# Scores of two items in every second slot, with 6 and 10 MLP pieces by turns

## The chip, the cores and the metric

The kernel runs on one core of one Trainium2 chip. The time is the device time of one execution in microseconds (us): 1641.6 us before, the median of 3 runs (1641.4 to 1641.78). The core has five engines that run side by side, each through its own list of instructions in order: TensorE (PE, matmuls; PEld are its weight loads), VectorE (DVE), ScalarE (ACT), GpSimd (POOL) and SyncE (SP, DMA issues). They wait for each other by semaphores. Matmul results land in PSUM[...]; ScalarE or VectorE copies them on to SBUF.

## The reference, cut to what matters

Attention that keeps only the 32 largest scores of each row, over 8 batches, 8 heads, 576 positions and a head size of 64, and then an MLP with exact gelu on the 4608 resulting rows. Everything is fp32.

```python
def _attn_ref(q, k, v):                       # (8, 8, 576, 64) each
    scores = scale * np.matmul(q, k.transpose(0, 1, 3, 2))
    kth = np.partition(scores, -32, axis=-1)[..., -32:-31]
    scores = np.where(scores >= kth, scores, -1e9)
    scores = scores - np.max(scores, axis=-1, keepdims=True)
    attn = np.exp(scores)
    attn = attn / (np.sum(attn, axis=-1, keepdims=True) + 1e-09)
    return np.matmul(attn, v)

# x = attention output as (4608, 512)
def _moe_ref(x, w_in, w_out):                 # (512, 2048), (2048, 512)
    h = x @ w_in
    g = 0.5 * h * (1.0 + erf(h / np.sqrt(2.0)))
    return g @ w_out
```

## The kernel before

The attention is cut into 144 items. An item is 128 query rows of two heads; 18 items make a batch, and two of these 18 hold the last 64 rows of the heads. The main loop has one slot for each item (and four more), and the stages of an item lie in successive slots:

- its scores: matmuls into `t_ps` (the last 64 keys of both heads) and `s_ps` (the first 512 keys, two banks), and ScalarE copies both into the item's row tile `s`;
- two slots later the top 32 of each row on VectorE, four rounds of eight;
- in the slot after that the masked softmax on ScalarE (prelu, then exp with its sum), the inverse of the sum on VectorE and the normalising on GpSimd;
- in the slot after that the transposes on TensorE, which ScalarE copies to `pt`; and for every second item one slot later the product with v (`o`), for both items at once.

The MLP is cut into 1152 pieces, each four recorded matmuls into `h_ps` (first layer) or two into `y_ps` (second layer), and these pieces are laid between the attention's work. `block` gives eight pieces of one layer, and blocks of the layers alternate. A gelu of two tiles follows each block of the second layer. The excerpts are in the order of the file; `...` marks cuts.

```python
    def scores(i):
        ...
        S_of[i] = s = work.tile([P, 2 * S], f32, tag="s", bufs=5, name="s")
        s_ps = ps.tile([P, 2, 512], f32, tag="s", bufs=1, name="s_ps")
        t_ps = ps.tile([P, 512], f32, tag="tp", name="t_ps")      # two buffers of tag "tp"
        if t < NM:
            ...
            nc.tensor.matmul(t_ps[:, 0:P], lhsT=lhsT, rhs=qk[:, SM + P : KT], start=True, stop=True)
            for c in range(2):
                for e in range(2):
                    ...                        # 64 rows of the array: one head each
                    nc.tensor.matmul(s_ps[:, e, c * 256 : (c + 1) * 256], ...)
            ...
            nc.scalar.activation(spread(s, S + TL, SM), s_ps, func=AF.Copy, scale=scale)
            nc.scalar.activation(s[:, SM : S + TL], t_ps[:, 0:P], func=AF.Copy, scale=scale)
        ...

    def top_k(i, hooks):
        ...
        for r in range(TOPK // 8):
            for e in range(2):
                nc.vector.max(st["top"][:, e, 8 * r : 8 * r + 8], cur[e])
            if r < TOPK // 8 - 1:
                ...                            # match_replace, both heads
            if r in hooks:
                hooks.pop(r)()
    ...
    def softmax(i, e):
        ...
        nc.scalar.activation(s, s, func=AF.Prelu, bias=st["neg"][:, e, 1:2], scale=1.0, alpha=STEEP)
        nc.scalar.activation(s, s, func=AF.Exp, bias=st["bias"][:, e : e + 1], scale=1.0,
                             accum_out=st["den"][:, e : e + 1])

    def transposes(i):
        ...
        def tails():                           # reads the ends of both heads' rows
            ...
                nc.tensor.transpose(tp[:, 0:P], s[:, SM : S + TL], ident)
                nc.scalar.copy(out=pt_now[0][:, 2 * NM, ...], in_=tp[:, 0:P])
        def main(e):                           # four transposes of one head's row
            ...
            nc.scalar.copy(out=dst, in_=tp.rearrange("p (j n) -> p j n", j=NM))

        return [tails] + [lambda e=e: main(e) for e in range(2)]
```

The loop over the slots. `mlp(k)` issues up to k pieces, as long as the slot's allowance `left[0]` lasts. `prep` are transposes that prepare q and k of a later pair of heads; not all slots have them.

```python
    ahead = N + 4                              # N = 144 items
    for n in range(ahead):
        left[0] = 4 if n in (START, START + 1) else 8        # START = 10
        ...
        scores(n + 2)
        product = attend(n - 3)                # o: product with v, for every second item
        late = n > START
        ...
        copy_x()                               # ScalarE copies o
        mlp(1)
        tr = transposes(n - 2)
        if product and n > START and ...:      # the next piece needs the rows of this product
            for piece in tr[:1]:
                piece()
            tr, ready[0] = tr[1:], n_tok[0]
        if n > START:
            softmax(n - 1, 0)
        mlp(1)
        ...
        mlp(1)
        prep = prep_in.pop(n, [])
        if len(prep) > 1 and len(tr) == 3:
            tr, prep = tr[:1] + prep[:1] + tr[1:], prep[1:]
        for piece in tr[:-1]:                  # tails and the first main
            piece()
            ready[0] = n_tok[0]
            mlp(1)
        ...
        if late:
            softmax(n - 1, 1)
        add_small(n - 1)                       # GpSimd: den + 1e-9
        ...
        for piece in tr[-1:] + prep:           # the second main, preparation
            piece()
            mlp(1)
        run_gelus()
        mlp(left[0])                           # what is left of the allowance
        run_gelus()
        if n < N:
            top_k(n, {3: lambda: inverse(n - 1)})     # VectorE: 1/den behind the top-k
        ...
        threshold(n)                           # GpSimd: neg, bias
        ...
        normalise(n - 1, 2 if on_pool(u) else 0)      # GpSimd, both heads; VectorE in a few early slots
```

Of the kernel before, what the change touches and what calls it, by code (L numbers as in the profile page):

```python
# [14 lines left out]
def kernel(  # L15
# [6 lines left out]
    w_out: bass.AP,  # L22
    out: bass.AP,
):

# [7 lines left out]
    nc = tc.nc  # L35
    f32, i32, u32 = mybir.dt.float32, mybir.dt.int32, mybir.dt.uint32
    bf16, i16, u16 = mybir.dt.bfloat16, mybir.dt.int16, mybir.dt.uint16
    AF = mybir.ActivationFunctionType
    ALU = mybir.AluOpType

    B, H, S, D = q.shape
    P = 128
# [3 lines left out]
    NP = H // 2  # L46
    NM = S // P
    SM = NM * P
    TL = S - SM
# [174 lines left out]
    N = len(items)  # L224
# [35 lines left out]
    def spread(t, step, n):  # L260

        return bass.AP(tensor=t.tensor, offset=t.offset, ap=[list(t.ap[0]), [step, 2], [1, n]])

    def half(r, e):


        return slice((r ^ e) * TL, ((r ^ e) + 1) * TL)
# [2 lines left out]

        return spread(t[:, e * TL :], step + (TL if e == 0 else -TL), TL)

    def scores(i):
        if i >= N:
            return
        pair, t = items[i]
        S_of[i] = s = work.tile([P, 2 * S], f32, tag="s", bufs=5, name="s")
        s_ps = ps.tile([P, 2, 512], f32, tag="s", bufs=1, name="s_ps")
        t_ps = ps.tile([P, 512], f32, tag="tp", name="t_ps")
        if t < NM:  # L280
            qk = qk_of[pair]
            lhsT = qk[:, t * P : (t + 1) * P]
            nc.tensor.matmul(t_ps[:, 0:P], lhsT=lhsT, rhs=qk[:, SM + P : KT], start=True, stop=True)  # L283
            for c in range(2):
                for e in range(2):
                    rows = slice(e * D, (e + 1) * D)
                    nc.tensor.matmul(  # L287
                        s_ps[:, e, c * 256 : (c + 1) * 256], lhsT=lhsT[rows, :],
                        rhs=qk[rows, KT + c * 256 : KT + (c + 1) * 256], start=True, stop=True,
                    )  # L290
            if i == 0:

                nc.scalar.activation(s[:, 0:SM], s_ps[:, 0], func=AF.Copy, scale=scale)  # L293
                nc.vector.tensor_scalar(s[:, SM : S + TL], t_ps[:, 0:P], scale, None, op0=ALU.mult)
                nc.scalar.activation(s[:, S + TL :], s_ps[:, 1], func=AF.Copy, scale=scale)  # L295
                return
            nc.scalar.activation(spread(s, S + TL, SM), s_ps, func=AF.Copy, scale=scale)  # L297
            nc.scalar.activation(s[:, SM : S + TL], t_ps[:, 0:P], func=AF.Copy, scale=scale)
        else:
            for r in range(2):  # L300
                qk = qk_of[pair + r]
                for e in range(2):
                    nc.tensor.matmul(
                        t_ps[half(r, e), r * TL : (r + 1) * TL],
                        lhsT=qk[:, SM + e * TL : SM + (e + 1) * TL],
                        rhs=qk[:, SM + P + e * TL : SM + P + (e + 1) * TL],
                        start=True, stop=True,
                    )

            for r in range(2):  # L310
                qk = qk_of[pair + r]
                for e in range(2):
                    rows = slice(e * D, (e + 1) * D)
                    nc.tensor.matmul(  # L314
                        s_ps[half(r, e), r, :], lhsT=qk[rows, SM + e * TL : SM + (e + 1) * TL],
                        rhs=qk[rows, KT:], start=True, stop=True,
                    )
            s2 = s.rearrange("p (r n) -> p r n", r=2)
            nc.scalar.activation(s2[:, :, 0:SM], s_ps, func=AF.Copy, scale=scale)
            nc.scalar.activation(  # L320
                s2[:, :, SM:S], t_ps[:, 0:P].rearrange("p (r n) -> p r n", r=2),
                func=AF.Copy, scale=scale,
            )

    def top_k(i, hooks):

# [47 lines left out]
    def softmax(i, e):  # L374

        if i < 0 or i >= N:
            return
        st, s = stat_of[i], row(i, e)
        nc.scalar.activation(s, s, func=AF.Prelu, bias=st["neg"][:, e, 1:2], scale=1.0, alpha=STEEP)  # L379
        nc.scalar.activation(  # L380
            s, s, func=AF.Exp, bias=st["bias"][:, e : e + 1], scale=1.0,
            accum_out=st["den"][:, e : e + 1],
        )
# [56 lines left out]
    def copy_x():  # L440
        while copies:
            copies.pop()()

    n_tok, read = [0], [0]

    copies = []

    def attend(i):

        if i < 0 or i >= N:  # L450
            return False
        pair, t = items[i]
        b, at = divmod(pair, NP)
        if t < NM and t % 2 == 0:
            return False
        pt = pt_now[0]
        o = ps.tile([P, 512], f32, tag="tp", name="o")
        n, row = (2 * P, (t - 1) * P) if t < NM else (TL, SM)
        tok = place_of(b, row)
        assert read[0] >= tok + n - RING  # L460
        c = slice(tok % RING, tok % RING + n)
        if t < NM:
            vt = raw_of("v", pair)
            for j in range(NJ):
                for e in range(2):
                    nc.tensor.matmul(  # L466
                        o[e * D : (e + 1) * D, 0:n], lhsT=vt[:, j, e, :],
                        rhs=pt[:, e * NM + j if j < NM else 2 * NM, :],
                        start=(j == 0), stop=(j == NJ - 1),
                    )  # L470
            copies.append(lambda: nc.scalar.copy(out=xT[:, at, c], in_=o[:, 0:n]))
        else:
            for r in range(2):
                vt = raw_of("v", pair + r)
                for j in range(NJ):
                    for e in range(2):
                        nc.tensor.matmul(  # L477
                            o[e * D : (e + 1) * D, r * TL : (r + 1) * TL], lhsT=vt[:, j, e, :],
                            rhs=pt[:, r, j, half(r, e)], start=(j == 0), stop=(j == NJ - 1),
                        )  # L480
            copies.append(lambda: nc.scalar.copy(
                out=xT[:, at : at + 2, c],
                in_=o[:, 0 : 2 * TL].rearrange("p (r n) -> p r n", r=2),
            ))

        if t == (NM if b % 2 == 0 else NM - 1):
            for r in range(2 if t == NM else 1):
                load("v", pair + r + NP + 1)
        if at == (NP - 1 if t < NM else NP - 2):
            assert n_tok[0] == tok  # L490
            n_tok[0] = tok + n
        return True

# [135 lines left out]
    for pair in range(2):  # L631
        for piece in transpose_qk(pair, pair == 0):
            piece()
        if pair == 0:
            scores(0)
            scores(1)

# [6 lines left out]
    for pair in range(2, n_pairs):  # L646
        b, p = divmod(pair, NP)
        for at, piece in zip(first.get(pair, slots_of[b % 2][p]), transpose_qk(pair)):
            prep_in.setdefault(starts[b] + at, []).append(piece)
    ahead = N + 4  # L650
    for n in range(ahead):

        left[0] = 4 if n in (START, START + 1) else 8
        eager[0] = n > N
        weights_add(unit_in(n))
        scores(n + 2)
        product = attend(n - 3)
        late = n > START
        if n <= START:

            softmax(n - 1, 0)
        copy_x()
        mlp(1)
        tr = transposes(n - 2)
        if product and n > START and done[0] < len(pieces) and pieces[done[0]][0] > ready[0]:

            for piece in tr[:1]:
                piece()
            tr, ready[0] = tr[1:], n_tok[0]
        if n > START:  # L670
            softmax(n - 1, 0)
        mlp(1)
        if not late:
            softmax(n - 1, 1)
# [4 lines that stand above are left out]
        for piece in tr[:-1]:  # L679
# [6 lines that stand above are left out]
        add_small(n - 1)  # L686
        if ends_late(unit_in(n)):
            weights_end(unit_in(n))
        for piece in tr[-1:] + prep:
# [4 lines that stand above are left out]
        mlp(left[0])  # L694
        run_gelus()
        if n < N:
            top_k(n, {3: lambda: inverse(n - 1)})
        else:
            inverse(n - 1)
        threshold(n)  # L700
        u = unit_in(n + 1)

        normalise(n - 1, 2 if on_pool(u) else 0)

        weights_size(unit_in(n + 1))
        if n >= FIRST:
            load_weights(n + 2)
        if n <= NP:
            load("v", n)
# [38 lines left out]
```

## Time and profile before

The profile is of one execution on the chip. Times of single instructions are in us from the start of the span. A line of a timeline has the start, the duration, the engine, the source line, the operation, the tile it writes and the tiles it reads, their sizes and how often; in brackets stands how long the engine was idle before it and what ended that.

| what | value | how to read it |
|---|---|---|
| span of the profiled execution | 1640.4 us | first to last instruction |
| TensorE busy | 1589.1 us (97%) | ends are modelled, so a busy TensorE is not one at its peak |
| VectorE busy | 1415.4 us (86%) | MAX8 at 747 ns and MATCH_REPLACE8 at 743 ns, 14 in a slot |
| ScalarE busy | 1185.5 us (72%) | with 68 + 67 table loads of 1283 ns for gelu and exp |
| GpSimd busy | 662.3 us (40%) | 476.5 us of it the normalising, 278 rows at 1723 ns |
| mean granted TensorE clock | 0.979 | full speed in all but the first slices |
| `y_ps` matmuls | 548.9 us, x1152 | MLP, second layer |
| `h_ps` matmuls | 553.0 us, x2560 | MLP, first layer |
| `tp` matmuls | 178.5 us, x1152 | transposes of the normalised rows |
| `o` matmuls (128x256) | 155.6 us, x1280 | product with v |
| `s_ps` matmuls (64x256) | 152.9 us, x1024 | scores of the first 512 keys |
| evictions of `s_ps` | 1027 ns, x127 | ScalarE, two banks at once |

Each fp32 matmul of the program shows as two records, each transpose as one.

### The profile page before, as it was taken

How to read it: one execution, taken by the hardware profiler on the slowest of the kernel's cores; microseconds unless marked ns; L12 is line 12 of the kernel's file. 1: busy time of each engine (PE TensorE's matmuls, PEld its weight loads, DVE VectorE, ACT ScalarE, POOL GpSimd, SP SyncE). 2: the span in 40 equal slices, each digit the busy share in tenths (PEclk: the TensorE clock that was granted, in tenths of full speed). 3: DMA queues.
4: the chain of work that ended last, by engine and by line, in shares of the span. 5: the costliest groups of instructions: out<-in, count | busy, mean ns of one | idle time of the engine just before them, and what ended most of it. 6: DMA issues, size and time to landing. Idle time of an engine off the chain costs nothing.

```text
span 1640.4 us, 25030 instructions
## 1 busy us (share of the span) xinstructions
PE 1589.1 (97%) x8818; PEld 1077.1 (66%) x8818; DVE 1415.4 (86%) x3046; ACT 1185.5 (72%) x2133; POOL 662.3 (40%) x759
## 2 busy tenths in 40 slices
PE   6669999999999999999999999999999999999999
PEld 4346676766666666676666667676666666666665
DVE  8999999988898989998989898998889888999800
ACT  6999877777777777777777777777777777777720
POOL 4888633333333333333333233333333333333300
PEclk7679999999999999999999999999999999999999
DMA  6433210011101110001110111001110101000000
GB/s 164 139 108 127 55 43 1 14 29 44 35 1 28 30 47 12 7 22 36 29 28 14 30 30 43 1 14 31 42 36 1 28 16 35 1 14 2 6 13 13
DMA packets 126765, 56.14 MB, mean 34 GB/s; under 512 B 117776, under 2 KB 118064, under 8 KB 126640
## 3 DMA queue, kind: packets, MB, share of 16 engines
q1 hardware_dynamic: 125376, 54.12, 12.3%
q8 instruction: 70, 1.15, 0.3%
q14 instruction: 55, 0.45, 0.1%
q10 hardware_dynamic: 1200, 0.39, 0.1%
q0 software_dynamic: 64, 0.03, 0.0%
HBM read 45.08 MB, written 9.44 MB: 33 GB/s over the span
## 4 chain that ended last, share of the span: by engine, by line
PE 92%; ACT 5%; issue 1%; DMA 1%; DVE 1%; POOL 0%; SPq 0%; ACTq 0%; DVEq 0%; POOLq 0%
PE y_ps L554 30%; PE h_ps L518 30%; PE o L466 9%; PE tp L429 8%; PE s_ps L287 8%; PE tp_qk L242 2%; PE t_ps L283 2%; PE o L477 1%; ACT s L380 1%; PE s_ps L314 1%; ACT s L379 1%; PE tp_t L411 1%; ACT s L297 1%; ACT w_out_sb L179 1%; ACT w_in_sb L175 1%
## 5 line engine op out<-in xcount | busy, mean ns | idle before, releaser
L340 DVE MAX8 top<-rest 128x8 f32<-128x576 f32 x864 | 609.5, 747 | 0.0
L518 PE MATMUL h_ps<-xT,w_in_sb 128*128 128x256 f32 (+1 forms) x2560 | 553.0, 361 | 0.0
L554 PE MATMUL y_ps<-w_out_sb,g 128*128 128x512 f32 x1152 | 548.9, 599 | 0.0
L392 POOL TENSOR_SCALAR s<-s,rden 128x576 f32<-128x576 f32 x278 | 476.5, 1723 | 0.6 <-DVE rden L366 0.4
L518 PEld LDWEIGHTS h_ps<-xT,w_in_sb 128*128 128x128 f32 x2560 | 428.4, 191 | 61.8 <-issue 16.8
L343 DVE MATCH_REPLACE8 rest<-top,rest 128x576 f32<-128x576 f32 x576 | 423.4, 743 | 0.0
L372 POOL TENSOR_SCALAR den<-den 128x2 f32<-128x2 f32 x144 | 32.0, 222 | 838.4 <-ACT s L380 837.9
L554 PEld LDWEIGHTS y_ps<-w_out_sb,g 128*128 128x128 f32 x1152 | 195.1, 190 | 168.2 <-issue 167.3
L297 ACT ACTIVATE s<-s_ps 128x1024 f32<-128x1024 f32 x127 | 130.4, 1027 | 165.7 <-PE s_ps L287 143.8
L380 ACT ACTIVATE s<-s,bias 128x576 f32<-128x576 f32 x288 | 223.4, 776 | 13.2 <-ACT s L379 0.7
L379 ACT ACTIVATE s<-s,neg 128x576 f32<-128x576 f32 x288 | 224.1, 778 | 0.3 <-POOL neg L355 0.2
L436 ACT COPY pt<-tp 128x512 f32<-128x512 f32 x256 | 147.1, 574 | 102.2 <-PE tp L429 102.2
L429 PEld LDWEIGHTS tp<-ident,s 128*128 128x128 f32 x1152 | 145.9, 144 | 102.1 <-issue 58.9
L343 DVE MATCH_REPLACE8 rest<-top,s 128x576 f32<-128x576 f32 x288 | 211.7, 743 | 0.0
L340 DVE MAX8 top<-s 128x8 f32<-128x576 f32 x288 | 201.8, 742 | 1.4 <-ACT s L293 1.4
L429 PE MATMUL tp<-ident,s 128*128 128x128 f32 x1152 | 178.5, 279 | 15.1 <-ACT pt L412 12.1
L466 PE MATMUL o<-pt,raw_v 128*64 128x256 f32 x1280 | 155.6, 390 | 0.0
L287 PE MATMUL s_ps<-qk 64*128 64x256 f32 x1024 | 152.9, 419 | 0.8 <-ACT s L295 0.8
L366 DVE RECIPROCAL rden<-den 128x2 f32<-128x2 f32 x144 | 23.2, 161 | 139.4 <-POOL den L372 139.1
L466 PEld LDWEIGHTS o<-pt,raw_v 128*64 128x64 f32 x1280 | 87.8, 139 | 66.1 <-issue 23.6
L287 PEld LDWEIGHTS s_ps<-qk 64*128 64x128 f32 x1024 | 92.4, 195 | 24.0 <-issue 2.0
L529 ACT ACTIVATE g<-h_ps 128x512 f32<-128x512 f32 x144 | 78.6, 595 | 37.8 <-PE h_ps L518 37.1
(71 smaller groups left out, 1075.8 us busy)
## 6 DMA issues: line engine op xcount, KB each, us to landing
raw_q<-in_q_dram SPq DMA_DIRECT2D x64, 128.0 KB, 2.4
raw_v<-in_v_dram SPq DMA_DIRECT2D x64, 128.0 KB, 2.5
w_out_sb<-in_moe_w_in_dram SPq DMA_DIRECT2D x16, 511.8 KB, 4.9
raw_k<-in_k_dram SPq DMA_DIRECT2D x62, 128.0 KB, 2.5
out_dram<-y SPq DMA_DIRECT2D x31, 256.0 KB, 2.2
w_out_sb<-in_moe_w_out_dram SPq DMA_DIRECT2D x10, 511.8 KB, 4.1
words<-in_moe_w_out_dram SPq DMA_DIRECT2D x6, 511.8 KB, 4.6
out_dram<-y SPq DMA_DIRECT2D x9, 128.0 KB, 2.3
```

The costliest lines, as they stand in the source:

```text
L287: nc.tensor.matmul(s_ps[:, e, c * 256 : (c + 1) * 256], lhsT=lhsT[rows, :], rhs=qk[rows, KT + c * 256 : KT + (c + 1) * 256], start=True, s ...
L297: nc.scalar.activation(spread(s, S + TL, SM), s_ps, func=AF.Copy, scale=scale)
L340: nc.vector.max(st["top"][:, e, 8 * r : 8 * r + 8], cur[e])
L343: nc.vector.match_replace(rest[:, e], st["top"][:, e, 8 * r : 8 * r + 8], cur[e], LOWEST)
L379: nc.scalar.activation(s, s, func=AF.Prelu, bias=st["neg"][:, e, 1:2], scale=1.0, alpha=STEEP)
L380: nc.scalar.activation(s, s, func=AF.Exp, bias=st["bias"][:, e : e + 1], scale=1.0, accum_out=st["den"][:, e : e + 1],)
L392: (nc.vector if e >= 2 - on_dve else nc.gpsimd).tensor_scalar(s, s, st["rden"][:, e : e + 1], None, op0=ALU.mult)
L429: nc.tensor.transpose(tp[:, j * P : (j + 1) * P], s[:, first + j * P : first + (j + 1) * P], ident)
L436: nc.scalar.copy(out=dst, in_=tp.rearrange("p (j n) -> p j n", j=NM))
L466: nc.tensor.matmul(o[e * D : (e + 1) * D, 0:n], lhsT=vt[:, j, e, :], rhs=pt[:, e * NM + j if j < NM else 2 * NM, :], start=(j == 0), stop= ...
L518: nc.tensor.matmul(h_tile(u)[:, i, :], lhsT=w_in_sb[:, ko, f * P : (f + 1) * P], rhs=xT[:, ko, c0 : c0 + n], start=(ko == 0), stop=(ko == ...
L554: nc.tensor.matmul(y_of[sub], lhsT=g_of[u][:, i, sub * P : (sub + 1) * P], rhs=w_out_sb[:, f, :], start=(f == 0), stop=(f == FT - 1),)
```

## The change

From slot 22 on (the constant `PAIRED` is 20, and slot 21 is the first odd one without scores) the even slots make the scores of two items, n+1 and n+2, and the odd slots make none. Both items' `t_ps` share one PSUM tile; its two parts are computed and evicted first, then the first item's `s_ps`; the product with v comes between the first and the second item's `s_ps`, and the second eviction is issued behind the first half of the softmax. The allowance of pieces becomes 6 in even slots, which have the product as well, and 10 in odd slots. The aim is that TensorE has about the same work in both kinds of slot, and changes less often between kinds of matmul.

```diff
-    def scores(i):
-        if i >= N:
-            return
+    def last_scores(i, t_ps):
...
+            nc.tensor.matmul(
+                t_ps, lhsT=qk[:, t * P : (t + 1) * P], rhs=qk[:, SM + P : KT], start=True, stop=True
+            )
...
+    def main_scores(i):
...
+        s_ps = ps.tile([P, 2, 512], f32, tag="s", bufs=1, name="s_ps")
...
+        return lambda: nc.scalar.activation(dst, s_ps, func=AF.Copy, scale=scale)
+
+    def scores(ids, between):
+        ids = [i for i in ids if i < N]
...
+        t_ps = ps.tile([P, 512], f32, tag="tp", name="t_ps")
+        for x, i in enumerate(ids):
+            S_of[i] = work.tile([P, 2 * S], f32, tag="s", bufs=5, name="s")
+            last_scores(i, t_ps[:, x * P : (x + 1) * P])
+        first = ids == [0] or len(ids) > 1
+        if not first:
+            evict = main_scores(ids[0])
+            evict()
+        for x, i in enumerate(ids):
...
+                nc.scalar.activation(dst, src, func=AF.Copy, scale=scale)
+        if first:
+            main_scores(ids[0])()
+        between()
+        return main_scores(ids[1]) if len(ids) > 1 else lambda: None
...
+    PAIRED = START + 2 * NP + 2
     for n in range(ahead):
-        left[0] = 4 if n in (START, START + 1) else 8
+        left[0] = 4 if n in (START, START + 1) else 8 if n <= PAIRED else 6 if n % 2 == 0 else 10
         eager[0] = n > N
         weights_add(unit_in(n))
-        scores(n + 2)
-        product = attend(n - 3)
+        product = has_product(n - 3)
+        ids = [n + 2] if n <= PAIRED else [] if n % 2 else [n + 1, n + 2]
+        rest = scores(ids, lambda: attend(n - 3))
...
         if n > START:
             softmax(n - 1, 0)
+        rest()
         mlp(1)
```

The rest of the diff moves the test for a product out of `attend` into `has_product`, and calls `scores` with a list for the first two items.

More of the change, by code (lines that the diff above doesn't have):

```diff
@@ L271, in halves @@
         return spread(t[:, e * TL :], step + (TL if e == 0 else -TL), TL)
-    def scores(i):
-        if i >= N:
-            return
+    def last_scores(i, t_ps):
         pair, t = items[i]
-        S_of[i] = s = work.tile([P, 2 * S], f32, tag="s", bufs=5, name="s")
-        s_ps = ps.tile([P, 2, 512], f32, tag="s", bufs=1, name="s_ps")
-        t_ps = ps.tile([P, 512], f32, tag="tp", name="t_ps")
         if t < NM:
             qk = qk_of[pair]
-            lhsT = qk[:, t * P : (t + 1) * P]
-            nc.tensor.matmul(t_ps[:, 0:P], lhsT=lhsT, rhs=qk[:, SM + P : KT], start=True, stop=True)
+            nc.tensor.matmul(
+                t_ps, lhsT=qk[:, t * P : (t + 1) * P], rhs=qk[:, SM + P : KT], start=True, stop=True
+            )
+            return
+        for r in range(2):
+            qk = qk_of[pair + r]
+            for e in range(2):
+                nc.tensor.matmul(
+                    t_ps[half(r, e), r * TL : (r + 1) * TL],
+                    lhsT=qk[:, SM + e * TL : SM + (e + 1) * TL],
+                    rhs=qk[:, SM + P + e * TL : SM + P + (e + 1) * TL],
+                    start=True, stop=True,
+                )
+    def main_scores(i):
+        pair, t = items[i]
+        s = S_of[i]
+        s_ps = ps.tile([P, 2, 512], f32, tag="s", bufs=1, name="s_ps")
+        if t < NM:
+            qk = qk_of[pair]
             for c in range(2):
@@ L287, in scores @@
                     nc.tensor.matmul(
-                        s_ps[:, e, c * 256 : (c + 1) * 256], lhsT=lhsT[rows, :],
+                        s_ps[:, e, c * 256 : (c + 1) * 256], lhsT=qk[rows, t * P : (t + 1) * P],
                         rhs=qk[rows, KT + c * 256 : KT + (c + 1) * 256], start=True, stop=True,
                     )
[L291 to L298, printed above, removed]
-        else:
[L300 to L308, printed above, removed]
+            dst = spread(s, S + TL, SM)
+        else:
             for r in range(2):
@@ L317, in scores @@
                     )
[L318 to L323, printed above, removed]
+            dst = s.rearrange("p (r n) -> p r n", r=2)[:, :, 0:SM]
+        if i == 0:
+            return lambda: [
+                nc.scalar.activation(s[:, c : c + SM], s_ps[:, e], func=AF.Copy, scale=scale)
+                for e, c in ((0, 0), (1, S + TL))
+            ]
+        return lambda: nc.scalar.activation(dst, s_ps, func=AF.Copy, scale=scale)
+    def scores(ids, between):
+        ids = [i for i in ids if i < N]
+        if not ids:
+            between()
+            return lambda: None
+        t_ps = ps.tile([P, 512], f32, tag="tp", name="t_ps")
[7 more added lines that the diff above has]
+        for x, i in enumerate(ids):
+            s, src = S_of[i], t_ps[:, x * P : (x + 1) * P]
+            if items[i][1] < NM:
+                dst = s[:, SM : S + TL]
+            else:
+                dst = s.rearrange("p (r n) -> p r n", r=2)[:, :, SM:S]
+                src = src.rearrange("p (r n) -> p r n", r=2)
+            if i == 0:
+                nc.vector.tensor_scalar(dst, src, scale, None, op0=ALU.mult)
+            else:
+                nc.scalar.activation(dst, src, func=AF.Copy, scale=scale)
+        if first:
+            main_scores(ids[0])()
+        between()
+        return main_scores(ids[1]) if len(ids) > 1 else lambda: None
     def top_k(i, hooks):
@@ L442, in copy_x, with has_product @@
             copies.pop()()
+    def has_product(i):
+        return 0 <= i < N and (items[i][1] == NM or items[i][1] % 2 == 1)
     n_tok, read = [0], [0]
@@ L448, in attend @@
     def attend(i):
-        if i < 0 or i >= N:
-            return False
+        if not has_product(i):
+            return
         pair, t = items[i]
         b, at = divmod(pair, NP)
-        if t < NM and t % 2 == 0:
-            return False
         pt = pt_now[0]
@@ L491, in attend @@
             n_tok[0] = tok + n
-        return True
     g_of, y_of, h_of = {}, {}, {}
@@ L634 @@
         if pair == 0:
-            scores(0)
-            scores(1)
+            for i in range(2):
+                scores([i], lambda: None)
     slots_of = [
```

## The prediction

> **What bounds the kernel now.** I read the page first, then the chain of work that ended last in order of time, then the timeline of single slots. From the page:
>
> ```profile
> PE 1589.1 (97%) x8818; PEld 1077.1 (66%) x8818; DVE 1415.4 (86%) x3046; ACT 1185.5 (72%) x2133; POOL 662.3 (40%) x759
> ...
> PE 92%; ACT 5%; issue 1%; DMA 1%; DVE 1%; POOL 0%; SPq 0%; ACTq 0%; DVEq 0%; POOLq 0%
> ```
>
> TensorE is the bound: 92% of the chain is its own work. A busy TensorE could still hide pauses, so the chain inside slots 40 and 41 (start, us, what):
>
> ```profile
> 442.93 0.44 PE tp L429 x4
> 443.36 0.86 PE h_ps L518 x4
> 444.23 0.44 PE tp L429 x4
> 444.67 2.59 PE h_ps L518 x12
> 447.26 0.22 PE t_ps L283 x2
> 447.48 1.06 PE s_ps L287 x8
> 448.54 2.77 PE y_ps L554 x6
> 451.31 0.11 PE tp_t L411
> ```
>
> Here are the prices. One MLP piece (four records of `h_ps`, or two of `y_ps`) is 0.86 us; four transposes are 0.44 us, so 0.107 us each; the scores of an item are 0.22 + 1.06 us, of which about 0.1 us between `t_ps` and `s_ps` and 0.2 us behind `s_ps` are changes of operand shape and not streaming. From 230 us to the end of the top-k, 1325 us, I summed start to start what TensorE does and took off the streaming time: 1252 us stream, 72 us are such changes, and no single one is over 0.5 us. So TensorE is not once kept waiting there, except in slot 142, below. VectorE has a floor of 9.70 us a slot (the interval of most odd slots), TensorE needs about 21.6 us for two slots: 2 us of slack for VectorE in each pair.
>
> What keeps TensorE supplied is the way from an item's softmax to its transposes. Slot 40, from the first main transposes (start, duration):
>
> ```profile
> 442.76 0.60 PE L429 MATMUL tp<-ident,s 128*128 128x128 f32 x4
> ...
> 443.40 0.59 ACT L436 COPY pt<-tp 128x512 f32<-128x512 f32 x1 [0.75 <-PE tp L429]
> ...
> 443.88 0.78 ACT L379 ACTIVATE s<-s,neg 128x576 f32<-128x576 f32 x1
> ...
> 445.37 0.19 ACT L380 ACTIVATION_READ_ACCUMULATOR s<-s,bias 128x1 f32 x1
> ...
> 445.64 0.22 POOL L372 TENSOR_SCALAR den<-den 128x2 f32<-128x2 f32 x1 [7.89 <-ACT s L380]
> 445.90 0.17 DVE L366 RECIPROCAL rden<-den 128x2 f32<-128x2 f32 x1 [2.30 <-POOL den L372]
> ...
> 446.44 3.43 POOL L392 TENSOR_SCALAR s<-s,rden 128x576 f32<-128x576 f32 x2
> ...
> 451.15 0.27 PE L411 MATMUL tp_t<-ident,s 128*128 128x128 f32 x1
> ```
>
> ScalarE copies the first main transposes of item n-2 (443.40), then does the second half of the softmax of n-1 (to 445.56); GpSimd adds the small constant, VectorE inverts, GpSimd normalises both heads (to 449.87). Only then may TensorE start the tail transpose of n-1, in the next slot. From the first main transpose to the end of the normalising it is 449.87 - 442.76 = 7.11 us; I call this the loop. Most even slots show 7.10 or 7.11. TensorE comes to the tail transpose only after 8.39 us (451.15 - 442.76): 1.3 us to spare. Slot 142 has no scores, and so less work in between:
>
> ```profile
> 1541.27 0.60 PE L429 MATMUL tp<-ident,s 128*128 128x128 f32 x4
> ...
> 1544.95 3.43 POOL L392 TENSOR_SCALAR s<-s,rden 128x576 f32<-128x576 f32 x2
> ...
> 1545.60 2.74 PE L554 MATMUL y_ps<-w_out_sb,g 128*128 128x512 f32 x6
> ...
> 1548.43 0.14 PEld L411 LDWEIGHTS tp_t<-ident,s 128*128 128x128 f32 x1 [0.92 <-POOL s L392]
> ```
>
> There the distance is 1548.43 - 1541.27 = 7.16 us and the releaser is the normalising: TensorE waited. So 7.16 us is the least distance between the main transposes of one slot and the tail transpose of the next.
>
> [...] So a tail transpose that waits holds up the MLP pieces behind it; the trace agrees, in slot 142 the next matmul starts behind it (1548.60). [...] all distances here are start to start. [...] a row of normalising takes 1723 ns on GpSimd and 517 ns in the ten early ones on VectorE, so 3.4 of the 7.1 us of the loop are GpSimd's two rows.
>
> **The change, part by part.**
> *Removed and added work.* None: the same matmuls, evictions and pieces (6 + 10 = 8 + 8). Changes of shape: the order of an even slot becomes t, t, s, o, s, pieces; the odd one has no scores. One step from t to s (0.11 us) and the entry of an odd slot's scores (0.04) go. The change from o to h (0.17) becomes one from o to s, which before has nowhere; I take 0.2 from s to o. Sum -0.12 us a pair, times 62 pairs (even slots 22 to 144): -7.6 us.
>
> *Moved work, even to odd slot.* Before, between the main transposes of an even slot and the tail transpose of the odd one lie: four transposes (0.43), one piece, four transposes (0.43), three pieces, scores (1.38), three pieces, 0.1 for the change: 0.86 + 7 x 0.86 + 1.38 + 0.1 = 8.4, which is the measured 8.39. After, the even slot has two pieces left after the first main transposes, the odd slot has no scores and three pieces: 0.86 + 5 x 0.86 + 0.1 = 5.26 us. The loop still takes 7.16 us, for ScalarE is free in time: in the even slot its two small evictions, the big one, the copy of o (near 4.05 us after the slot's start), the first softmax half with its 1.28 us table load, the second big eviction and the tail copy end near 8.6 us; the first main transposes start at 8.7 and are copied at 9.34. So TensorE waits 7.16 - 5.26 = 1.90 us in each such pair. By the order of the changed kernel's instructions, with the prices above:
>
> - 22 even slots with no preparation transposes between: 1.90 us, 41.9
> - 6 with two transposes between (+0.21): 1.69 us, 10.1
> - 12 with four (+0.43): 1.47 us, 17.7
> - 6 where preparation goes ahead of the main transposes and a piece with it (4.61 and 4.83): 14.6
> - 3 beside the last rows of a sequence (6.51): 2.0
> - 13 where the tail transposes go ahead of the pieces (distance 7.0 to 7.4, three of 8.2). There ScalarE is late. Now prelu comes 2.05 us after the main transposes instead of 1.12 (loop 8.02 us in slot 30); the second big eviction (0.92) comes in between, and the tail transposes come 1.06 later while the main ones come 1.0 later: loop near 9.08, in the three 9.4. Waits: 21.4.
>
> Sum 107.6 us.
>
> *Odd to even slot.* That distance grows to 11 to 15 us; VectorE, which inverts only behind a whole top-k of 9.5 us, delivers about 17 us after the even slot's main transposes, and TensorE comes to it 7.16 + 1.0 + 13.7 = 21.9 us after. No wait.
>
> *The single buffer of the scores.* The second s of a slot waits until the first is evicted. Usually: s is done 1.6 us after the slot's start, evicted by 2.7, needed at 3.95. Where a block of output tokens ends, 17 times, both copies of y now stand ahead of the table load and the gelus: 0.7 + 1.3 + 1.0 + two small evictions 0.55 + 1.02 gives 4.6 us. I count 0.7 us each: 12 us.
>
> Sum: 1641.6 - 7.6 + 107.6 + 12 = 1753.6; I say 1750.
>
> **Rivals.**
> 1. *Only the changes of shape count.* If something made the normalised row come 2 us earlier, the pairs would run without waits: about 1634 us. For it: TensorE waits nowhere now. Against it: 7.10 us is repeated to 0.01 in slots of every kind, and nothing in the change touches that loop.
> 2. *Balance frees VectorE.* Even slots lose work, odd ones gain, so odd slots no longer sit at VectorE's 9.70 us. That would bring at best nothing beyond rival 1, as TensorE never waited for VectorE.
> 3. *The scores' single buffer binds in every pair*, if ScalarE is still busy with gelus when the slot starts: 0.5 to 1 us more in 62 pairs, 1780 to 1810 us. Against it: in most odd slots the gelus can start before the slot ends, for the pieces they wait for come early in it.
> 4. *ScalarE, later in the even slot, lengthens the loop everywhere.* For it: two evictions more stand ahead of the main copy there. Against it: its margin is 0.7 us by the durations of slots 40 and 41. If it came 0.3 us too late everywhere, that would add 19 us.
>
> **Range and chances.** The wait of 1.5 to 1.9 us rests on two measured numbers. Uncertain are the step from o to s (0 to 0.3 us, 12 us down or 6 up), the 13 late slots (7 us either way), the 17 block ends (12 us down, 10 up), and a shift of ScalarE. Range 1722 to 1778. Slower by over 2% (1674) would fail only if 70% of the waits were missing: 0.93; within 2% 0.05; faster 0.02.
>
> **What would show it.** Right: TensorE idles before `tp_t` with the normalising as releaser, about 60 times and 1.5 to 2 us each; the distance from main to tail transposes in even slots is 7.16 us; a pair takes near 23 us; VectorE's wait for `den` grows; TensorE's share falls to about 92%. Wrong: distances of 5.3 us, which would need a shorter loop, or waits before the second `s_ps` in every pair.

## The result and the profile after

The changed kernel takes 1762.3 us (median of 5 runs, 1760.3 to 1765.2) against 1641.6 us before: ratio 1.0739, 95% interval 1.0725 to 1.0754. It is slower by 7.4%. The profiled span grew from 1640.4 to 1757.9 us.

The page of the changed kernel: engines, then the chain that ended last by engine, then two groups of instructions (busy time, mean ns of one, idle time before them and what ended most of it). Line numbers are those of the changed kernel: L444 is the tail transpose (L411 before), L462 the main transposes (L429), L425 the normalising (L392).

```profile
PE 1597.9 (91%) x8818; PEld 1067.7 (61%) x8818; DVE 1412.0 (80%) x3046; ACT 1191.9 (68%) x2133; POOL 663.4 (38%) x759
...
PE 61%; ACT 20%; POOL 15%; issue 2%; DVE 1%; DMA 1%; SPq 0%; POOLq 0%; ACTq 0%; DVEq 0%
...
L399 DVE RECIPROCAL rden<-den 128x2 f32<-128x2 f32 x144 | 22.5, 156 | 258.6 <-POOL den L405 258.6
...
L444 PE MATMUL tp_t<-ident,s 128*128 128x128 f32 x128 | 39.7, 310 | 107.4 <-POOL s L425 104.3
```

No engine got more work: the busy times are those of before within 1%. But the chain, 92% TensorE before, now is 61% TensorE, 20% ScalarE and 15% GpSimd: the end is reached through waits. The last line names the place: TensorE was idle for 104.3 us ahead of tail transposes, waiting for the normalising on GpSimd (14.6 us before the change, all of it in the first 105 us). VectorE's wait for `den` grew from 139.1 to 258.6 us, as a result.

The chain of slots 40 and 41 in order of time (start, us, what):

```profile
459.58 0.86 PE h_ps L551 x4
460.44 0.45 PE tp L462 x4
460.90 0.02 issue
460.92 0.59 ACT pt L469
461.51 0.68 ACT s L412
...
462.21 0.88 ACT s L413 x2
463.09 0.08 issue
463.17 0.22 POOL den L405
...
463.99 3.42 POOL s L425 x2
467.40 0.04 issue
467.45 0.33 PE tp_t L444
467.78 0.86 PE y_ps L587 x2
```

Before the change the same stretch was TensorE from end to end. Now the chain leaves TensorE with the first main transposes, goes through the copy, the second softmax half, the constant and 3.4 us of normalising, and comes back to TensorE at the tail transpose. The timeline shows what TensorE did meanwhile:

```profile
460.28 0.60 PE L462 MATMUL tp<-ident,s 128*128 128x128 f32 x4
...
462.02 2.76 PE L551 MATMUL h_ps<-xT,w_in_sb 128*128 128x256 f32 x12
...
463.96 3.43 POOL L425 TENSOR_SCALAR s<-s,rden 128x576 f32<-128x576 f32 x2
...
464.61 1.02 PE L587 MATMUL y_ps<-w_out_sb,g 128*128 128x512 f32 x2
...
467.45 0.33 PE L444 MATMUL tp_t<-ident,s 128*128 128x128 f32 x1 [1.81 <-POOL s L425]
```

From main to tail transposes it is 467.45 - 460.28 = 7.17 us, and the last piece in between started at 464.61 and streamed for 0.86 us: TensorE had nothing from 465.47 on, 1.98 us, of which the profile counts the 1.81 after the modelled end. The same 7.16 or 7.17 us stands in 45 of the 61 even slots from 22 to 142; the others are the slots with late ScalarE (ten of 8.98, three of 8.94) and three beside the last rows (6.74).

Where the time is, from the starts of TensorE's matmuls, one by one, less their streaming time (the commonest step from one start to the next among full-array matmuls of one size: 429 ns for 512 columns, 216 for 256, 109 for 128), from 230 us to the end: 64.7 us of changes and waits before, 184.1 us after, 119.4 more. Ahead of tail transposes 98.7; what follows the first tail transpose starts later, 5.1; ahead of preparation transposes in late slots 4.4; waits for the single score buffer 12.3; first-layer pieces that wait for a gelu in slots 21 to 28, 3.6; changes of shape -11.0, 260 of 0.18 us instead of 315; small ones 6.3.

The wait for the score buffer, at the end of a block of output tokens (start of slot 32), with the releaser in brackets:

```profile
357.63 0.59 ACT L594 COPY y<-y_ps 128x512 f32<-128x512 f32 x1 [2.85 <-PE y_ps L587]
...
358.24 1.28 ACT L562 ACT_TABLE_LOAD   x1
...
359.53 1.08 ACT L562 ACTIVATE g<-h_ps 128x512 f32<-128x512 f32 x2
...
360.82 1.06 ACT L325 ACTIVATE s<-s_ps 128x1024 f32<-128x1024 f32 x1
...
361.93 1.13 PE L303 MATMUL s_ps<-qk 64*128 64x256 f32 x8 [0.52 <-ACT s L325]
```

The second `s_ps` starts when the first one's eviction ends (361.88). The copy of y stood ahead of the table load and the gelus on ScalarE, so the eviction came late.

### The profile page after: what moved, and what is told of

It reads as the page before. It is cut to its first block, busy times and chain, and to the rows that moved or that the text cites. A ratio compares the mean times of both kernels' runs of the same rounds, so it can differ in the third digit from the quotient of the medians.

```text
span 1757.9 us, 24847 instructions
## 1 busy us (share of the span) xinstructions
PE 1597.9 (91%) x8818; PEld 1067.7 (61%) x8818; DVE 1412.0 (80%) x3046; ACT 1191.9 (68%) x2133; POOL 663.4 (38%) x759
## 4 chain that ended last, share of the span: by engine, by line
PE 61%; ACT 20%; POOL 15%; issue 2%; DVE 1%; DMA 1%; SPq 0%; POOLq 0%; ACTq 0%; DVEq 0%
PE y_ps L587 24%; PE h_ps L551 14%; POOL s L425 12%; PE o L500 6%; PE s_ps L303 6%; PE tp L462 5%; ACT s L413 5%; ACT s L412 4%; ACT pt L469 2%; ACT s L325 2%; PE tp_t L444 2%; ACT L562 1%; ACT g L562 1%; PE t_ps L279 1%; PE tp_qk L243 1%
## 5 line engine op out<-in xcount | busy, mean ns | idle before, releaser
L425 POOL TENSOR_SCALAR s<-s,rden 128x576 f32<-128x576 f32 x278 | 477.1, 1725 | 0.6 <-DVE rden L399 0.4
L587 PEld LDWEIGHTS y_ps<-w_out_sb,g 128*128 128x128 f32 x1152 | 203.4, 194 | 134.3 <-issue 131.1
L399 DVE RECIPROCAL rden<-den 128x2 f32<-128x2 f32 x144 | 22.5, 156 | 258.6 <-POOL den L405 258.6
L462 PEld LDWEIGHTS tp<-ident,s 128*128 128x128 f32 x1152 | 146.4, 144 | 102.1 <-issue 70.7
L462 PE MATMUL tp<-ident,s 128*128 128x128 f32 x1152 | 178.8, 279 | 14.1 <-ACT pt L445 11.6
L325 ACT ACTIVATE s<-s_ps 128x1024 f32<-128x1024 f32 x143 | 145.5, 1018 | 34.7 <-PE s_ps L303 31.0
L444 PE MATMUL tp_t<-ident,s 128*128 128x128 f32 x128 | 39.7, 310 | 107.4 <-POOL s L425 104.3
L500 PEld LDWEIGHTS o<-pt,raw_v 128*64 128x64 f32 x1280 | 87.9, 139 | 66.1 <-issue 21.6
L445 ACT COPY pt<-tp_t 128x128 f32<-128x128 f32 x128 | 33.3, 260 | 137.6 <-PE tp_t L444 136.8
```

What stands on the lines that cost most here:

```text
L325: return lambda: nc.scalar.activation(dst, s_ps, func=AF.Copy, scale=scale)
L425: (nc.vector if e >= 2 - on_dve else nc.gpsimd).tensor_scalar(s, s, st["rden"][:, e : e + 1], None, op0=ALU.mult)
L462: nc.tensor.transpose(tp[:, j * P : (j + 1) * P], s[:, first + j * P : first + (j + 1) * P], ident)
L500: nc.tensor.matmul(o[e * D : (e + 1) * D, 0:n], lhsT=vt[:, j, e, :], rhs=pt[:, e * NM + j if j < NM else 2 * NM, :], start=(j == 0), stop= ...
L587: nc.tensor.matmul(y_of[sub], lhsT=g_of[u][:, i, sub * P : (sub + 1) * P], rhs=w_out_sb[:, f, :], start=(f == 0), stop=(f == FT - 1),)
```

## The experiments

The theory (A): the way from the first main transposes of an even slot through softmax, inverse and normalising to the tail transpose of the next slot takes 7.17 us, and the change left only 5.19 us of TensorE work in between (465.47 - 460.28; the prediction and the expectations below count 5.26). Rivals: (B) the scores in pairs cost, by later evictions and the single score buffer; (C) the uneven division of the pieces costs as such. The table gives all runs; ratios are to the kernel before, with their 95% intervals.

| kernel | us | ratio | interval |
|---|---|---|---|
| after | 1762.3 | 1.0739 | 1.0725 to 1.0754 |
| pairs, 8 and 8 pieces | 1650.1 | 1.0056 | 1.0041 to 1.0071 |
| no pairs, 6 and 10 pieces | 1674.9 | 1.0207 | 1.0192 to 1.0222 |
| after, one row on VectorE | 1679.2 | 1.0234 | 1.0219 to 1.0249 |
| before, one row on VectorE | 1642.9 | 1.0013 | 1.0007 to 1.0020 |
| after, tails three pieces later | 1678.2 | 1.0228 | 1.0211 to 1.0245 |
| the same, pairs from slot 30 on | 1655.7 | 1.0087 | 1.0073 to 1.0101 |
| after, gelus earlier | 1751.2 | 1.0668 | 1.0653 to 1.0683 |
| pairs, 8 and 8, tails later, gelus earlier | 1652.5 | 1.0068 | 1.0055 to 1.0082 |
| pairs, 8 and 8, tails later, gelus ahead of y | 1664.3 | 1.0135 | 1.0120 to 1.0150 |
| tails later from 30, gelus ahead of y | 1666.4 | 1.0146 | 1.0129 to 1.0164 |
| before, tails joined to main transposes | 1640.7 | 1.0001 | 0.9993 to 1.0009 |

**Each part of the change alone.** In the changed kernel, 8 pieces everywhere:

```diff
-        left[0] = 4 if n in (START, START + 1) else 8 if n <= PAIRED else 6 if n % 2 == 0 else 10
+        left[0] = 4 if n in (START, START + 1) else 8
```

> The changed kernel with 8 pieces in every slot: scores in pairs, nothing moved between slots. Theory A (the wait is the way from the main transposes of an even slot through softmax, inverse and normalising to the tail transpose of the next slot, 7.17 us, against the TensorE work that lies in between): the work in between rises by two pieces from 5.26 to 6.97 us, so most pairs wait 0.2 us, six wait 0.6 to 0.8; with the waits for the single score buffer at block ends left: about 1655 to 1665 us. Theory B (scores in pairs are what costs, by later evictions on ScalarE and the single score buffer, and the division of the pieces is of no account): 1740 us or more. Theory C (uneven pieces are what costs, whatever the scores do): 1642 us.

And in the kernel before, 6 and 10 pieces:

```diff
-        left[0] = 4 if n in (START, START + 1) else 8
+        left[0] = 4 if n in (START, START + 1) else 8 if n <= START + 2 * NP + 2 else 6 if n % 2 == 0 else 10
```

> The kernel before with 6 and 10 pieces by turns from slot 21 on, scores one item a slot as before. Theory A: 6.67 to 7.07 us of work in between instead of 8.4 to 8.8, so 0.1 to 0.5 us of wait in most pairs: about 1655 to 1665 us. Theory B: 1642 us. Theory C: 1740 us or more.

Measured: pairs alone +0.6%, the division alone +2.1%, both together +7.4%. Neither B nor C can be the cause, for each says that one part alone has nearly the whole loss. A says why the parts do not add up: each takes work out of the same stretch, which had 1.3 us to spare. Behind slots 40 and 42 the pairs alone leave 6.91 us, the division alone 6.67, both 5.19; the tail transposes come at 7.16 or 7.17 us in all three.

The division alone was slower than A expected (1655 to 1665) by 10 us. There is a wait of another kind, which the expectation did not have. Its timeline at the end of slot 32:

```profile
363.06 0.60 PE L429 MATMUL tp<-ident,s 128*128 128x128 f32 x4
...
363.68 0.78 ACT L380 ACTIVATE s<-s,bias 128x576 f32<-128x576 f32 x1
...
364.46 0.56 ACT L436 COPY pt<-tp 128x512 f32<-128x512 f32 x1
...
365.07 0.49 PE L283 MATMUL t_ps<-qk 128*128 128x128 f32 x2 [0.33 <-ACT pt L436]
```

With only six pieces nothing is left behind the preparation transposes; the next scores come at once and want one of the two PSUM buffers that all transposes, products and `t_ps` share, before ScalarE, busy with the softmax, has copied the main transposes out of it. By start to start these waits are 13.8 us in 24 slots. The changed kernel has no scores in the slot that follows, and so not this wait.

**The way made shorter, TensorE's order as it is.** In even slots VectorE normalises the second head:

```diff
-        normalise(n - 1, 2 if on_pool(u) else 0)
+        normalise(n - 1, 2 if on_pool(u) else 1 if n > PAIRED and n % 2 == 0 else 0)
```

> The changed kernel, but in even slots VectorE normalises the second head's row (0.52 us) while GpSimd does the first (1.72 us). TensorE's order and pieces stay. Theory A: the way shrinks by about 1.7 us to near 5.45 us, against 5.26 us of work in between: the waits before the tail transposes fall from about 95 us in all to under 12, time 1660 to 1672 us. Theories B and C: TensorE's order is the same, so 1762 us.

Measured 1679.2 us: 83 us of the 121 are gone, though TensorE's order is untouched. Its timeline in slot 40:

```profile
450.25 0.60 PE L462 MATMUL tp<-ident,s 128*128 128x128 f32 x4
...
453.66 0.52 DVE L425 TENSOR_SCALAR s<-s,rden 128x576 f32<-128x576 f32 x1
...
453.75 0.48 POOL L391 TENSOR_TENSOR bias<-neg 128x2 f32<-128x2 f32 x1
...
454.21 1.72 POOL L425 TENSOR_SCALAR s<-s,rden 128x576 f32<-128x576 f32 x1
...
455.99 0.33 PE L444 MATMUL tp_t<-ident,s 128*128 128x128 f32 x1 [0.38 <-POOL s L425]
```

The tail transpose now comes at 5.74 us. I had expected 5.45 for the way; GpSimd's tiny `bias` took 0.48 us instead of 0.20 while VectorE normalised, and the row behind it began that much later. So 0.55 us of wait, from start to start, are left in most pairs without preparation transposes; from 230 us on the waits ahead of tail transposes are 21.6 us instead of 99.0, where under 12 were expected, and the time is 7 us over the range.

The counterpart is the same edit in the kernel before:

> The kernel before, with the second head's row normalised on VectorE in even slots from 22 on: the same shortening of the way by 1.4 us that brought 83 us in the changed kernel. Theory A: before the change 8.4 us and more of TensorE work lie in between, the way of 7.1 us is hidden, and shortening it brings nothing but the 0.2 us waits of slots 142 and 144: 1640 to 1642 us. Rival (normalising on GpSimd costs in any case): 1600 us or less.

Measured ratio 1.0013: nothing gained, 2 us lost. The way did shrink to 5.68 us there, but 8.39 us of work lie over it. The same 1.4 us are worth 83 us in one kernel and nothing in the other. This is the clearest of the runs.

**More work in between.** In odd slots three more of the ten pieces go ahead of the tail transposes:

```diff
-        mlp(1)
+        mlp(4 if n > PAIRED and n % 2 else 1)
         prep = prep_in.pop(n, [])
```

> The changed kernel, but in odd slots three pieces more are issued ahead of the tail transposes (6 instead of 3, of the same 10). Theory A: 7.83 us of work in between instead of 5.26, over the 7.17 us of the way: no wait before the tail transposes any more, 1648 to 1660 us, what is left being the waits for the score buffer at block ends less the changes of shape saved. Theory B and C: 1762 us, as the scores and the division of the pieces between slots are the same.

Measured 1678.2 us. The waits that A is about are gone: ahead of tail transposes behind y there is 0.1 us left of 99.0, from 230 us on. The time is 18 us over A's range, because of something else, which the waits of this run show (waiter, releaser: us in total, times, longest; the first line lies wholly in the first 105 us):

```profile
PE tp_t L444 <- POOL s L425: 17.5, 7, 4.5
...
PE h_ps L551 <- ACT g L562: 14.1, 4, 4.2
```

Four times a first-layer piece waits for a gelu, 3.5 to 4.3 us over the step itself, all in slots 21 to 28. Until slot 28 a block of the first layer begins inside an odd slot; the later order brings its first piece ahead of ScalarE's gelus. So the pairs were begun at slot 30 (`PAIRED = START + 2 * NP + 10`):

> The kernel with the tail transposes three pieces later, but the pairs begin at slot 30 instead of 22. Its four pauses of 3.5 to 4.4 us (first-layer matmuls waiting for a gelu) and the smaller ones behind them all lie in slots 21 to 28, where a block of the first layer begins inside the odd slot. If they come from that phase, they go and the time is 1655 to 1662 us; if they come from the later tail transposes, they turn up in other slots and the time stays near 1678 us.

Measured 1655.7 us, inside the range: the four pauses came from that phase.

**The score buffer.** In the changed kernel, the gelus earlier:

```diff
-    GELU_AT = 5
+    GELU_AT = 3
```

> The changed kernel with the gelus issued after the fourth piece of a second-layer block instead of the sixth, so that at block ends they stand ahead of the copies of y on ScalarE. Theory A with its side cost (16 waits for the score buffer before the second s_ps, 12.4 us over the step itself): these 16 waits go or fall under 0.1 us each, the waits before the tail transposes stay: 1747 to 1753 us. Rival (the second s_ps waits for its own first eviction, whatever the gelus do): 1762 us.

Measured 1751.2 us, 11 us less, and the 60 steps from o to s fall from 18.3 to 6.0 us in all, without one wait, while 98.9 us stay ahead of the tail transposes. So this side cost is 11 to 12 us, and independent of the large one.

**Is there a version that beats the kernel before?** With all waits gone the pairs would save 11 us of changes of shape (the first expectation here counts 5). The run with 8 and 8 pieces already has this saving (10.9 us) and loses it again: 9.6 us ahead of tail transposes and 1.9 behind, 4.4 ahead of preparation transposes, 3.5 for the score buffer. First, 8 and 8 pieces, `mlp(2 ...)` in odd slots at the place of the last but one diff, and `GELU_AT = 3`:

> Scores in pairs with 8 pieces in every slot, one piece more ahead of the tail transposes in odd slots (7.83 us of work in between, over the way of 7.17) and the gelus two pieces earlier. Theory A: no wait before the tail transposes and nearly none for the score buffer; what is left is the 4 us before the preparation transposes and 5 us saved in changes of shape: 1638 to 1643 us, as before the change. Rival (pairing has a cost of its own that no division mends): 1648 us or more.

Measured 1652.5 us: a miss. The waits ahead of tail transposes are gone, but with more pieces earlier in the odd slot both copies of y stand ahead of the gelus again, and the second `s_ps` waits 23 times by more than 0.2 us, 15 us in all. So the gelus were issued at the copies of y themselves:

```diff
         if f == FT - 1:
+            run_gelus()
             y, y_ps = work.tile([P, DM], f32, tag="y", name="y"), y_of.pop(sub)
```

> Scores in pairs, 8 pieces in every slot, one piece more ahead of the tail transposes in odd slots, and at block ends the gelus issued directly ahead of the copies of y. In the run with earlier gelus the score buffer still held up 23 second s_ps, 15 us over the step itself, since both copies of y stood ahead of the gelus again. Theory A: these waits go, and the time falls by 11 to 15 us to 1637 to 1642 us. Rival (the pairs have a cost of their own): 1650 us.

> 6 and 10 pieces from slot 30 on, three pieces more ahead of the tail transposes in odd slots, gelus ahead of the copies of y at block ends. Theory A: 1655.7 less some 11 to 13 us of waits for the score buffer: 1642 to 1646 us. Rival: 1656 us. If this one is below 1640 us, the division of 6 and 10 has a gain once its waits are gone; nothing seen so far speaks for it.

Measured 1664.3 and 1666.4 us: both worse than without. The first of them, around the end of slot 39:

```profile
432.82 1.28 ACT L562 ACT_TABLE_LOAD   x1
...
434.12 1.09 ACT L562 ACTIVATE g<-h_ps 128x512 f32<-128x512 f32 x2
435.09 0.59 ACT L595 COPY y<-y_ps 128x512 f32<-128x512 f32 x1
435.55 0.62 ACT L247 COPY qk<-tp_qk 128x512 f32<-128x512 f32 x1
...
436.22 0.49 PE L279 MATMUL t_ps<-qk 128*128 128x128 f32 x2 [2.41 <-ACT qk L247]
```

The gelus went ahead of the copy of the preparation transposes, for which the next `t_ps` waits: 2.4 us here, and as much in two more places. Of the 15 us for the score buffer only 4 went. ScalarE takes all of this in one order, here table load, gelus and the copy for `t_ps` (432.82, 434.12 and 435.55 us), and each order that I tried made TensorE wait somewhere. No version faster than the kernel before was found; of the runs with pairs the plain one with 8 and 8 pieces is the best.

Last, what was read as a small pause of 0.1 us ahead of each tail transpose in the kernel before: no MLP piece between tail and main transposes.

```diff
-        for piece in tr[:-1]:
+        for x, piece in enumerate(tr[:-1]):
             piece()
             ready[0] = n_tok[0]
-            mlp(1)
+            if x > 0 or len(tr) != 3:
+                mlp(1)
+        if len(tr) == 3:
+            mlp(1)
```

> The kernel before, scores one item a slot, 8 pieces each; the tail transpose directly ahead of the first four main transposes, without an MLP piece between. The reading behind it: TensorE has no waits, only changes of shape, and about 0.1 us of them stands before each single tail transpose but none before the four main ones. If the change is paid once for the group: 12 us less at most, 1629 to 1638 us. If the pause belongs to the tail transpose itself, wherever it stands: 1641 us.

Measured ratio 1.0001: nothing gained. The reading behind the run was wrong. The merged line of the six `y_ps` in the kernel before hides where the 0.1 us is; the starts of the weight loads show it:

```profile
448.47 2.84 PE L554 MATMUL y_ps<-w_out_sb,g 128*128 128x512 f32 x6
...
449.01 0.19 PEld L554 LDWEIGHTS y_ps<-w_out_sb,g 128*128 128x128 f32 x1 [0.24 <-issue]
449.44 0.19 PEld L554 LDWEIGHTS y_ps<-w_out_sb,g 128*128 128x128 f32 x1 [0.24 <-issue]
...
450.72 0.14 PEld L411 LDWEIGHTS tp_t<-ident,s 128*128 128x128 f32 x1 [0.24 <-issue]
...
451.15 0.27 PE L411 MATMUL tp_t<-ident,s 128*128 128x128 f32 x1
```

The six matmuls start at 448.47, 449.01, 449.44, 449.86, 450.29 and 450.72, the second and later ones together with these loads. The second comes 0.53 us after the first; all others, and the tail transpose, come 0.43 us after the one before. So no pause stands ahead of the tail transpose. The 0.1 us is the second half of the change of shape behind the scores: in the traces before and after, a change between full-array matmuls and the scores costs about 0.1 us ahead of the first matmul of the new shape and 0.1 us ahead of the second. Joining the tail to the main transposes leaves both (0.53 us between the first two `y_ps` there too).

## Why the prediction was right

1750 us were predicted and 1762 measured, inside the range, by the mechanism that was predicted.

- *The distance.* 7.16 us were taken from one wait in slot 142 of the kernel before, 5.26 us from counting pieces in the changed order. The tail transposes come at 7.16 or 7.17 us in the pairs without late ScalarE; shortening the way and lengthening the work each take the wait away, so this is shown. The 5.26 has one step too many: its 0.1 us "for the change" belongs to the scores (the last experiment) and goes with them. The work left is 5.19 us, the wait 1.98 instead of 1.90.
- *The sum of waits*, 107.6 us: 98.7 ahead of tail transposes, 5.1 behind and 4.4 ahead of preparation transposes, 108.2. That it agrees this well is partly luck. The 46 slots of the first four lines were put at 84.3 us and have 86.6; the late slots were put at 21.4 and have 13.4. Of these 8 us, 4.4 went to waits ahead of preparation transposes in the same slots, which the sum did not have, as it did not have the 5.1 behind. The tail transposes of the late slots came at 8.98 us where 9.08 was worked out. The slots beside the last rows came too high: their two tail transposes read one head each, so the first waits for one normalised row only (6.74 and 8.94 us instead of 7.16 and 9.4).
- *The score buffer*, 12 us from 17 waits of 0.7: 16 waits, 12.3 us. Thirteen of them exceed the step itself by 0.58 us, three by 1.58.
- *Changes of shape*, -7.6: -11.0. A step from t to s was priced at 0.11 us from merged lines; matmul by matmul it is 0.10 ahead of the first s and 0.10 ahead of the second, and one such step goes in each pair. From o to s it is 0.20, as assumed.
- *Missing in the sum*: gelus in slots 21 to 28 (3.6) and small pauses (6.3, part of them from two stretches at half clock, below). The changes of shape, which saved 3.4 us more than predicted, make up for a third of that; 3.6 us of the 12 were given away by rounding 1753.6 down.
- *Rivals.* The first would have needed a way of 5.2 us. The second was wrong: odd slots do not leave VectorE's floor. 59 of the 60 from 23 on begin 9.70 or 9.71 us before the next (29 of 60 before the change, where the prediction says most), since VectorE catches up after its long wait in the even ones; TensorE does not wait for it. The third (score buffer in every pair) did not come; the fourth neither, ScalarE's copy follows the main transposes after 0.64 us as before.

## What to carry to other kernels

When work is moved between stages of a software pipeline, the total on the bounding engine says little; for each dependence that leaves this engine and comes back, compare the time that the way takes with the engine's own work in between, before and after, from start to start. A slack that no profile of idle time shows (1.3 us in each 21.5) is used up by two moves that are each harmless. Moving one operation forward in an engine's order pushes another one back (the gelus ahead of y: 1664.3 us instead of 1652.5), so look at what that one releases. And a pause is where single instructions start late: in lines that merge several of them it can seem to stand ahead of the wrong one.

## What the runs showed of the hardware

**Half clock after a wait.** After 115 us the kernel before runs at full TensorE clock to the end of its matmuls (granted clock 1.00 from 116 to 1640 us). Behind the same 115 us the changed kernel has two stretches of 3.41 us at half clock (0.50), from 611.13 and from 1430.33 us; the first of them, of TensorE alone:

```profile
606.55 1.02 PE L587 MATMUL y_ps<-w_out_sb,g 128*128 128x512 f32 x2
609.81 0.33 PE L444 MATMUL tp_t<-ident,s 128*128 128x128 f32 x1 [2.24 <-POOL s L425]
609.98 1.02 PE L587 MATMUL y_ps<-w_out_sb,g 128*128 128x512 f32 x2
...
611.40 1.91 PE L587 MATMUL y_ps<-w_out_sb,g 128*128 128x512 f32 x2
```

And in the stretches around it (the columns here are the window, its length, busy us and instructions of PE, PEld, DVE, ACT and POOL, granted clock, DMA share, GB/s):

```profile
605.00:609.00 4.00, 2.57 (x10) 1.54 (x9) 3.21 (x8) 2.94 (x7) 3.30 (x5) 1.00 0.44 100
611.20:614.40 3.20, 3.20 (x10) 1.95 (x9) 3.20 (x8) 2.32 (x5) 0.22 (x1) 0.50 0.00 0
616.00:620.00 4.00, 4.00 (x25) 1.74 (x23) 4.00 (x10) 1.62 (x5) 3.60 (x3) 1.00 0.02 4
```

The pause was 2.24 us by the profile, the half clock came 1.3 us after its end and made the same two matmuls take 1.91 us instead of 1.02. Not every such pause was followed by it: of three pauses of 2.62 us (start to start less streaming) in this trace, the one from 1426.85 to 1429.47 us was followed by half clock, those from 582.29 and 1005.41 were not. What decides between them was not shown.

**VectorE beside GpSimd.** In the run with one row on VectorE, GpSimd's 128x2 subtraction took 0.48 us instead of 0.20 while VectorE normalised a row of 576. It ended at 454.23 us, 0.05 us behind VectorE's row. Beside VectorE's MAX8 the same operation took 0.20 us (463.79 us in the changed kernel). Why was not tried.
